# Ninety-six unused bytes at the right end of SBUF: an adaLN attention and MLP block on one core

## The chip, the core and the metric

The kernel runs on one core of a Trainium2 chip. A core has a matrix engine (TensorE, PE in the profile, with its weight loads shown apart as PEld), a vector engine (VectorE, DVE), a scalar engine (ScalarE, ACT), GpSimd (POOL) and SyncE (SP), which here issues nearly all transfers. They share an on-chip memory, SBUF, with 128 partitions; a tile takes the same bytes of every partition, so its address is a number of bytes from the start of a partition. Matrix products are accumulated in PSUM.

The metric is the device time of one execution, in microseconds (us). The kernel before takes 1168.71 us (median of three runs, 1167.72 to 1171.38).

## What is computed

There are 2048 tokens of width 576 (`x`, float32). A conditioning vector `c` gives six modulation rows. The block is linear attention with 32 heads of 18, followed by an MLP with a hidden width of 4608:

```
sa, ca, ga, sb, cb, gb = split(silu(c) @ w_mod)
h = layernorm(x) * (1 + ca) + sa
q, k, v = heads(h @ wqkv);  pq, pk = phi(q), phi(k)     # phi(t) = (t + 1 if t > 0 else exp(t)) + 1e-6
o = (pq @ (pk^T v)) / (pq @ sum(pk) + 1e-6)
x = x + ga * (o @ wo)
h = layernorm(x) * (1 + cb) + sb
x = x + gb * (silu(h @ w1) @ w2)
```

## The kernel before

**Arithmetic.** A float32 operand is kept as two parts, a rounded one (`fp32r`) and the rest, and each product takes three matmuls (high by high, high by low, low by high). PE does nearly nothing else.

**Stages.** The first stage (to about 240 us) makes the modulation, normalises and transposes `x` into the tiles `hT`, and projects K, V and half of Q, 128 tokens at a time; the weights of Q stand in the tile `wq`. The second (to about 400 us) finishes Q, applies the attention and does the first 256 hidden columns of the MLP in the plain way. The third, the main loop, does the other 17 groups of 256 hidden columns: `g` goes from 1 to 17, and for each `g` there are two units, `pair` 0 and 1, of 1024 tokens each. A short tail closes the last unit.

**A unit of the main loop.** Up and down products are done by a scheme with seven block products instead of eight. `ORDER = (1, 6, 2, 5, 7, 3, 4)` (L842) is the order of the seven. For each of them `passes` (L1211) does six matmuls, each with 128 stationary columns of a weight tile (`w`) and 512 moving columns (tokens) of an operand; products 2, 5, 3 and 4 have two more, whose stationary operand is the weights of the last 64 rows (`wt`). So there are groups of six and groups of eight. Between them stand the products of the down side, of 288 moving columns (L1284), twelve after most groups. DVE adds what they give to the accumulators (L1292), and POOL, ACT and DVE make the next operands.

**Where the moving operands come from.** Some stay in SBUF: in `hT` tiles, and, for products 7 and 3 of pair 1, in the two tiles `S`. Ten products of each `g` are streamed instead: they were stored to DRAM in tiles `hd`, and `fetch` (L968) reads each back into one of three rooms in turn. Two rooms are slices of `hT` tiles; the third is the tile `room` (L1425).

```
for room, m in rooms0.get(i) or [(rooms[(i + 2) % 3], left)]:                                  # L967
    nc.sync.dma_start(f32(room[:, :m, :]), hd[q, n][:, len(parts) : len(parts) + m, :])        # L968
...
T.matmul(ps, left, right, start=first and m == 0, stop=m == len(seq) - 1, ...)                 # L1211
```

**The tail weights.** `wts[g % 2]` holds `wt`. For odd `g` both parts lie in the tile `wtb` (L991). For even `g` they lie in the tile `wta` (L1155) and in a slice of a weight tile, which the profile calls `w`.

**Two sides of SBUF.** Pools are stacked from the left end of SBUF upwards, or, with `side="right"`, from its right end downwards. In the kernel before, the compiled program's right end lies at byte 229,344, which is 1791 times 128 and 96 over. Five pools stand there at some time, and each tile's size is a multiple of 128 bytes, so that each begins 96 bytes past a multiple of 128:

| tile (pool, line) | bytes | begins at | read by PE as |
|---|---|---|---|
| `wq` (wq, L118) | 20,736 | 208,608 | moving operand, Q projection (L212) |
| `S`, two buffers (hTb, L1059) | 8,192 each | 212,960 and 221,152 | moving operand, products 7 and 3 of pair 1 |
| `wtb` (hTb, L991) | 2,048 | 210,912 | stationary operand, odd `g` |
| `tq`, two buffers (tq, L1015) | 2,048 each | 206,816 and 208,864 | not read by PE |
| `S` (hTc, L1020) | 8,192 | 202,720 | not in the main loop |
| `room` (rs, L1425) | 10,240 | 200,672 | moving operand, a third of the streamed products |

On the left, `hT` (59,008 and 79,488), the weights `w` (99,968), `wta` (146,048), `xn` (175,744), the two tiles `first` (185,984 and 194,176) and the down weights (127,616 and up) all begin at multiples of 128.

**Order of work.** PE's order is that of the program text. From the second `g` on, the order of all engines is that of the text; between, a written list of indices for each engine (`arrange`, `ORDERS`) fixes it. Waits come from the tiles: whoever writes a tile waits for the last readers of whatever stood at the same bytes.

Of the kernel before, what the change touches and what calls it, by code (L numbers as in the profile page):

```python
# [9 lines left out]
F32 = mybir.dt.float32  # L10
# [6 lines left out]
P = 128  # L17
# [5 lines left out]
def kernel(ctx: ExitStack, tc, A_x, A_wqkv, A_wo, B_x, B_w1, B_w2, c, w_mod, out):  # L23
# [90 lines left out]
    accp = tc.alloc_tile_pool(name="acc", bufs=1)  # L114
    hTa = tc.alloc_tile_pool(name="hTa", bufs=2)
    wp = tc.alloc_tile_pool(name="w", bufs=1)
    wg = tc.alloc_tile_pool(name="wg", bufs=2)
    wqp = tc.alloc_tile_pool(name="wq", bufs=1, side="right")  # L118
    pa = tc.alloc_tile_pool(name="pa", bufs=1)
    psA = tc.alloc_tile_pool(name="psA", bufs=1, space=PSUM)  # L120
# [1020 lines left out]
    w2p = tc.alloc_tile_pool(name="w2p", bufs=1, reuse_waits="tile")  # L1141
    pu = tc.alloc_tile_pool(name="pu", bufs=1, reuse_waits="tile")
    pf = tc.alloc_tile_pool(name="pf", bufs=1, reuse_waits="tile")
    ph = tc.alloc_tile_pool(name="ph", bufs=1, reuse_waits="tile")
# [8 lines left out]
    rs = tc.alloc_tile_pool(name="rs", bufs=1, side="right", reuse_waits="tile")  # L1153
# [293 lines left out]
            unit.plain_down(work)  # L1447
            run(tokens.split(), (unit, behind2), ())
    psC.release()
    for p in (rs, ph, pf, pu, w2p, wqp, wp, hTa, accp):  # L1450
        p.release()


# [26 lines left out]
```

## Time and profile before

| | before |
|---|---|
| median of the runs | 1168.71 us (1167.72 to 1171.38) |
| profiled execution, first to last instruction | 1167.7 us |
| its mean granted TensorE clock | 0.999 |
| PE busy | 1144.4 us, 98% |
| DVE busy | 977.4 us, 84% |
| POOL busy | 660.1 us, 57% |
| ACT busy | 531.2 us, 45% |
| transferred | 268.61 MB, 230 GB/s mean |

How to read it. The span is the time from the first to the last instruction of one profiled execution; no other time of that execution is shown. A line such as `up<-room,w` names the tiles by the program's names: what is written, and after the arrow what is read; `128*128 128x512` is a stationary tile of 128 by 128 and 512 moving columns. Matmuls overlap: the duration of one includes its way through the array, so what PE pays for each is the distance from one start to the next start. In the timeline, the first column is the start of a run of like instructions, the second the time from its first start to its last end, and xN their number.

### The profile page before, as it was taken

How to read it: one execution, taken by the hardware profiler on the slowest of the kernel's cores; microseconds unless marked ns; L12 is line 12 of the kernel's file. 1: busy time of each engine (PE TensorE's matmuls, PEld its weight loads, DVE VectorE, ACT ScalarE, POOL GpSimd, SP SyncE). 2: the span in 40 equal slices, each digit the busy share in tenths (PEclk: the TensorE clock that was granted, in tenths of full speed). 3: DMA queues.
4: the chain of work that ended last, by engine and by line, in shares of the span. 5: the costliest groups of instructions: out<-in, count | busy, mean ns of one | idle time of the engine just before them, and what ended most of it. 6: DMA issues, size and time to landing. Idle time of an engine off the chain costs nothing.

```text
span 1167.7 us, 19567 instructions
## 1 busy us (share of the span) xinstructions
PE 1144.4 (98%) x7203; PEld 1058.8 (91%) x7203; DVE 977.4 (84%) x1539; ACT 531.2 (45%) x1088; POOL 660.1 (57%) x749
## 2 busy tenths in 40 slices
PE   6899999999999999999999999999999999999998
PEld 6799999999998889999999999999999999999998
DVE  3857574478797899999999999999999999999996
ACT  3553433346556454444444454444444444444541
POOL 2500000164554387677677767757767776776686
PEclk9999999999999999999999999999999999999999
DMA  8303210022357879769769779688697697697684
GB/s 284 102 28 105 64 55 1 1 83 63 112 218 266 322 261 348 274 254 351 272 252 363 266 280 334 262 319 308 249 352 275 257 345 273 255 364 268 256 308 152
DMA packets 57231, 268.61 MB, mean 230 GB/s; under 512 B 5484, under 2 KB 19312, under 8 KB 34096
## 3 DMA queue, kind: packets, MB, share of 16 engines
q1 hardware_dynamic: 56964, 267.06, 62.2%
q8 instruction: 57, 0.93, 0.3%
q10 hardware_dynamic: 172, 0.30, 0.1%
q14 instruction: 38, 0.31, 0.1%
HBM read 250.56 MB, written 16.78 MB: 229 GB/s over the span
## 4 chain that ended last, share of the span: by engine, by line
PE 94%; DVE 2%; DMA 2%; ACT 1%; issue 0%; SPq 0%; DVEq 0%; ACTq 0%
PE up L1211 33%; PE down L1284 31%; PE psK L212 12%; PE big L212 7%; PE small L774 2%; PE big L785 2%; PE kvp L517 1%; PE kvp L329 1%; PE psK L668 1%; PE big L700 1%; DMA room<-hd 1%; DVE hT L109 1%; PE small L200 1%; DMA hT<-in_w_mod_dram 1%; PE up L1314 1%; PE down L1314 1%
## 5 line engine op out<-in xcount | busy, mean ns | idle before, releaser
L1292 DVE TENSOR_TENSOR acc<-down,acc 128x576 f32<-128x576 f32 x330 | 246.2, 754 | 14.1 <-PE down L1284 4.3
L1211 PE MATMUL up<-hT,w 128*128 128x512 f32 x916 | 240.3, 391 | 0.0
L1211 PEld LDWEIGHTS up<-hT,w 128*128 128x128 f32 x916 | 164.6, 188 | 25.8
L1246 POOL TENSOR_TENSOR s<-f,f 128x256 f32<-128x256 f32 x66 | 51.6, 782 | 163.9 <-ACT f L1227 163.9
L1284 PE MATMUL down<-w,hc 128*128 128x288 f32 x792 | 120.7, 294 | 0.0
L1284 PE MATMUL down<-w,hb 128*128 128x288 f32 x792 | 120.7, 294 | 0.0
L1284 PEld LDWEIGHTS down<-w,hb 128*128 128x128 f32 x792 | 113.5, 188 | 6.0 <-DVE U L1292 0.4
L1284 PEld LDWEIGHTS down<-w,hc 128*128 128x128 f32 x792 | 113.6, 188 | 5.6
L1292 DVE TENSOR_TENSOR U<-down,U 128x576 f32<-128x576 f32 x132 | 99.5, 754 | 18.0 <-PE down L1284 15.7
L109 DVE TENSOR_TENSOR w<-v,w 128x288 fp32r<-128x288 f32 (+1 forms) x170 | 111.8, 667 | 0.4 <-ACT w L954 0.4
L212 PE MATMUL psK<-w,hT 128*128 128x288 f32 (+2 forms) x660 | 108.0, 298 | 0.8 <-DVE w L287 0.6
L212 PEld LDWEIGHTS psK<-w,hT 128*128 128x128 f32 x660 | 95.0, 189 | 1.5 <-DVE w L287 0.8
L1211 PE MATMUL up<-room,w 128*128 128x512 f32 x348 | 93.2, 396 | 1.7 <-DMA room<-hd 1.7
L1265 POOL TENSOR_TENSOR hc<-s,hc 128x512 fp32r<-128x512 f32 x66 | 89.8, 1360 | 0.0
L1227 ACT ACTIVATE f<-f 128x512 f32<-128x512 f32 x102 | 64.4, 631 | 48.1 <-DVE f L1232 25.7
L1230 DVE TENSOR_TENSOR f<-up,p 128x512 f32<-128x512 f32 x102 | 69.7, 683 | 14.7 <-PE up L1211 10.1
L1211 PEld LDWEIGHTS up<-room,w 128*128 128x128 f32 x348 | 62.4, 188 | 13.0 <-DVE f L1232 2.1
L954 ACT CAST w<-v 128x288 fp32r<-128x288 f32 x85 | 36.5, 434 | 77.0 <-PE down L1284 52.1
L1250 POOL TENSOR_TENSOR f<-f,s 128x256 f32<-128x256 f32 x66 | 50.6, 767 | 34.4 <-DVE hb L1265 27.3
L1284 PE MATMUL down<-w,hd 128*128 128x288 f32 x396 | 63.2, 295 | 0.0
L1284 PE MATMUL down<-w,he 128*128 128x288 f32 x396 | 63.1, 295 | 0.0
L1284 PE MATMUL down<-w,ha 128*128 128x288 f32 x396 | 63.0, 294 | 0.0
(284 smaller groups left out, 2498.4 us busy)
## 6 DMA issues: line engine op xcount, KB each, us to landing
hT<-hd SPq DMA_DIRECT2D x66, 1280.0 KB, 5.8
hT<-hd SPq DMA_DIRECT2D x45, 1024.0 KB, 5.1
room<-hd SPq DMA_DIRECT2D x35, 1280.0 KB, 6.0
room<-hd SPq DMA_DIRECT2D x20, 1024.0 KB, 5.8
v<-in_B_w_dram SPq DMA_DIRECT2D x17, 576.0 KB, 7.3
v<-in_B_w_dram SPq DMA_DIRECT2D x17, 512.0 KB, 7.6
hd<-S SPq DMA_DIRECT2D x6, 1024.0 KB, 4.2
xt<-in_A_x_dram SPq DMA_DIRECT2D x16, 288.0 KB, 3.1
```

The lines of the kernel that those rows point to most:

```text
L109: return V.tensor_sub(lo, full, f32(hi))
L212: T.matmul(ps, xpart(a), wpart(b), start=n == 0, stop=n == len(XW) - 1)
L774: T.matmul(ps, left, right, start=n == 0, stop=n == len(seq) - 1)
L954: A.copy(self.w2[n][:, 0], src)
L1211: T.matmul(ps, left, right, start=first and m == 0, stop=m == len(seq) - 1, skip_group_check=True)
L1227: A.activation(self.f[i, k], self.f[i, k], AF.Silu)
L1230: V.tensor_add(f, self.bank[bank[1]], self.p1)
L1246: G.tensor_add(self.s[:, 0:1], half(i, 0, 1), half(i, 1, 1))
L1250: G.tensor_sub(half(i, 1, 0), half(i, 1, 0), self.s[:, 1:2])
L1265: eng.tensor_sub(t[:, :, 1, :], src, f32(t[:, :, 0, :]))
L1284: T.matmul(ps[:, p, :HALF], self.a[i, n][:, u, p * P : (p + 1) * P], self.w.w2[n][:, v], start=n in (1, 5, 7, 6) and j == 0, stop=j == 2, ...
L1292: V.tensor_add(dst, ps[:, :, :HALF], dst)
```

## The change

A pool `edge` is opened on the right side ahead of `wq`, with one tile of 24 float32 per partition (96 bytes) that nothing reads or writes, and it is released at the end.

```diff
     wg = tc.alloc_tile_pool(name="wg", bufs=2)
+    edge = tc.alloc_tile_pool(name="edge", bufs=1, side="right")
+    edge.tile([P, 24], F32, name="edge")
     wqp = tc.alloc_tile_pool(name="wq", bufs=1, side="right")
...
-    for p in (rs, ph, pf, pu, w2p, wqp, wp, hTa, accp):
+    for p in (rs, ph, pf, pu, w2p, wqp, edge, wp, hTa, accp):
         p.release()
```

Every tile of the right side moves down by 96 bytes: `wq` to 208,512, `S` to 212,864 and 221,056, `wtb` to 210,816, `tq` to 206,720 and 208,768, the third `S` to 202,624, `room` to 200,576. All are multiples of 128. Nothing moves on the left side, whose tiles end at 200,576 or lower while `room` stands, and no instruction is added or taken away.

## The prediction

> **What bounds the kernel now.** I read the page's busy times and its chain first, then the table of stages, then the groups by shape, and last the timeline of single products.
>
> ```profile
> PE 1144.4 (98%) x7203; PEld 1058.8 (91%) x7203; DVE 977.4 (84%) x1539; ACT 531.2 (45%) x1088; POOL 660.1 (57%) x749
> PE 94%; DVE 2%; DMA 2%; ACT 1%; issue 0%; SPq 0%; DVEq 0%; ACTq 0%
> ```
> ```profile
> core 0: us, PE busy (x) PEld busy (x) DVE busy (x) ACT busy (x) POOL busy (x), PEclk, DMA share, GB/s
> 330.00:417.00 87.00, 84.52 (x520) 76.11 (x519) 75.79 (x128) 48.45 (x92) 38.65 (x42) 1.00 0.78 291
> 417.00:700.00 283.00, 283.00 (x1680) 256.31 (x1679) 263.05 (x390) 130.82 (x283) 202.90 (x241) 1.00 0.78 291
> 700.00:1000.00 300.00, 300.00 (x1781) 272.09 (x1781) 278.75 (x411) 137.38 (x298) 215.66 (x255) 1.00 0.80 298
> ```
>
> PE is 94% of the chain that ends last. In the main loop it is busy in 283.00 of 283 us and in 300.00 of 300, at the full granted clock (1.00): it waits for nobody. DVE, next, is busy in 263.05 of the 283 us, 93%. So the time of this loop is the sum of the distances between matmul starts, and nothing else. A change that moves tiles without touching an instruction can win or lose time here only by changing those distances.
>
> Do they depend on the tile? The groups by shape give the duration of one matmul behind the bar, in ns:
>
> ```profile
> L1211 PE MATMUL up<-hT,w 128*128 128x512 f32 x916 | 240.3, 391 | 0.0
> L1284 PE MATMUL down<-w,hc 128*128 128x288 f32 x792 | 120.7, 294 | 0.0
> L1211 PE MATMUL up<-room,w 128*128 128x512 f32 x348 | 93.2, 396 | 1.7 <-DMA room<-hd 1.7
> L1211 PE MATMUL up<-S,w 128*128 128x512 f32 x204 | 53.1, 395 | 0.0
> L1211 PE MATMUL up<-hT,wtb 128*128 128x512 f32 x108 | 33.5, 391 | 0.0
> L1211 PE MATMUL up<-room,wtb 128*128 128x512 f32 x34 | 10.7, 395 | 0.0
> L1211 PE MATMUL up<-first,w 128*128 128x512 f32 x12 | 2.9, 390 | 0.0
> L1314 PE MATMUL down<-w2B,hc 128*128 128x288 f32 x12 | 2.3, 296 | 0.0
> ```
>
> With the moving operand in a tile of the left side (`hT`, `first`) one takes 390 to 391 ns; in a tile of the right side (`room`, `S`) 395 to 396. That a stationary `wtb` costs anything doesn't show in durations. What PE pays is the distance of starts, which the timeline of PE shows by groups:
>
> ```profile
> 703.06 1.53 PE L1211 MATMUL up<-hT,w 128*128 128x512 f32 x6
> 704.42 0.96 PE L1284 MATMUL down<-w,hb 128*128 128x288 f32 x6
> ...
> 706.00 1.57 PE L1211 MATMUL up<-room,w 128*128 128x512 f32 x6
> ...
> 707.87 0.95 PE L1284 MATMUL down<-w,hc 128*128 128x288 f32 x6
> ...
> 709.48 1.53 PE L1211 MATMUL up<-hT,w 128*128 128x512 f32 x6
> ...
> 711.30 0.96 PE L1284 MATMUL down<-w,ha 128*128 128x288 f32 x6
> ...
> 735.48 1.57 PE L1211 MATMUL up<-S,w 128*128 128x512 f32 x6
> 736.89 0.29 PE L1284 MATMUL down<-w,hb 128*128 128x288 f32 x1
> ...
> 754.70 1.54 PE L1211 MATMUL up<-hT,w 128*128 128x512 f32 x6
> ...
> 756.53 0.95 PE L1284 MATMUL down<-w,ha 128*128 128x288 f32 x6
> ...
> 758.12 1.56 PE L1211 MATMUL up<-room,w 128*128 128x512 f32 x6
> 759.51 1.74 PE L1284 MATMUL down<-w,hb 128*128 128x288 f32 x12
> ...
> 767.93 1.54 PE L1211 MATMUL up<-hT,w 128*128 128x512 f32 x6
> 769.31 0.96 PE L1284 MATMUL down<-w,hd 128*128 128x288 f32 x6
> ...
> 841.72 1.56 PE L1211 MATMUL up<-room,w 128*128 128x512 f32 x6
> 843.58 0.95 PE L1284 MATMUL down<-w,hc 128*128 128x288 f32 x6
> ```
>
> The time of a group is the start of the first down matmul behind it less its own start. Six from `hT`: 704.42 - 703.06 = 1.36 us. Six from `S`: 736.89 - 735.48 = 1.41; from `room`: 759.51 - 758.12 = 1.39. Eight with `hT` and `wta`: 711.30 - 709.48 = 1.82. Eight with `room` and `wta`: 707.87 - 706.00 = 1.87; with `room` and `wtb`: 843.58 - 841.72 = 1.86. Eight with `hT` and `wtb`, 756.53 - 754.70 = 1.83. The other groups of a kind repeat these within 0.02. So a right-side tile costs PE in either place, as moving and as stationary operand. The one property that all of them share, and no tile of the other kind has, is a start 96 bytes past a multiple of 128.
>
> **The change part by part.** What it removes is that remainder. It adds no instruction, no transfer and no wait: every pair of tiles that shared bytes before does so after (`room` now begins exactly where the left side ends, at 200,576, and shares nothing new). I go through the reads of the right side, with the price of an all-left group as what each comes to.
>
> *Groups of six on `room` or `S`.* Of the 55 transfers into `room` 20 carry 1024 KB, for a product of six; the other 35 carry 1280 KB, for one of eight. `S` serves product 7, of six, once for each of 17 values of `g`. That is 37 groups at 1.40 (the mean of 1.39 and 1.41) against 1.36: 37 x 0.04 = 1.5 us.
>
> *Groups of eight on `room` or `S`.* 35 by `room` and 17 by product 3 on `S`: 52 at 1.87 against 1.82: 52 x 0.05 = 2.6; the 26 of odd `g` are nearer 1.86, so 2.5.
>
> *Groups of eight on `hT` with `wtb`.* The 108 matmuls with `hT` and `wtb` stand in 54 groups; 9 of these move `S` in their first six and are counted above, and one group moves `xn`: 46 are left. At 1.83 to 1.85 against 1.82, 46 x 0.02 = 0.9.
>
> *What follows such a group.* An all-left six can be dear behind a right-side group: 769.31 - 767.93 = 1.38 against 1.36. I count some 25 of the 65 all-left sixes: 25 x 0.015 = 0.4. The twelve down matmuls behind an eight with `room` and `wta` take 709.48 - 707.87 = 1.61; those behind an all-left six take 706.00 - 704.42 = 1.58. There are 26 such (18 on `room`, 8 on `S`): 26 x 0.03 = 0.8, and I take off 0.2 for the down groups behind `wtb`, which are 3 ns quicker than the others now. Together 1.0.
>
> *`wq`.* The Q projection of 128 tokens is 28 matmuls of 288 columns that move `wq`; the K projection is the same with left-side weights.
>
> ```profile
> 140.05 3.89 PE L212 MATMUL psK<-wq,hT 128*128 128x288 f32 x28
> 143.78 0.43 PE L212 MATMUL psK<-w,hT 128*128 128x288 f32 x2
> ```
> ```profile
> 164.53 0.43 PE L212 MATMUL psK<-w,hT 128*128 128x288 f32 x2
> ...
> 168.26 0.60 PE L200 MATMUL psT<-ident,xt 128*128 128x128 f32 x4
> ```
>
> Q takes 143.78 - 140.05 = 3.73 and K 168.26 - 164.53 = 3.73, by 28. At 288 columns the remainder costs nothing, and I take 0. The bound: 16 such projections at 0.01 either way, 0.2.
>
> *The transfers.* The refills of `room` land 6.0 and 5.8 us after issue by the page, those of `hT` 5.8 and 5.1, so the right side may be slower for DMA too. But PE is never idle in the loop for want of a refill; the one place is the first use of `room`:
>
> ```profile
> 394.59 8.36 DMA room<-hd
> ...
> 403.09 1.64 PE L1211 MATMUL up<-room,w 128*128 128x512 f32 x6 [1.71 <-DMA room<-hd]
> ```
>
> There 1.71 us of idle could shrink by at most the 0.7 us of the larger difference. The transfer is long because others share the queue, so I take 0 and keep 0 to 0.7. The stores from `S` and the copies by ACT and DVE into right-side tiles lie in the 330 to 417 us stage; no pair of rows separates their side from their neighbours, and I take 0.
>
> The sum: 1.5 + 2.5 + 0.9 + 1.0 = 5.9 us. Against the profiled execution that is 1167.7 - 5.9 = 1161.8; its span lies 1.0 under the median of the runs shown, so for a median I write 1168.7 - 5.9 = 1162.8 us, 0.5% less. Bounds: from below, if only the difference of the durations were won, (348 + 204) x 5 ns = 2.8 us, as 396 or 395 goes to 391; I hold to the starts because in a loop where PE is never idle they are the time. From above, 5.9 + 0.7 + 0.2 = 6.8.
>
> Does the gain reach the end? DVE would have to fill: 263.05 us in a stretch that shrinks from 283 to about 280.7 is 94%. The next bound lies 20 us away, the gain is 2.3.
>
> One rule speaks against the change. The Trainium skill, "SBUF — State Buffer", section "Specifications (TRN2)", gives SBUF lines of 16 bytes, with a penalty for each crossing to a new line. 96 is six such lines, so by that rule a start with remainder 96 is as good as one with remainder 0, and the sum would be 0 instead of 5.9 us. By that rule the first rival below is what happens; the trace so far disagrees, with 395 to 396 ns against 390 to 391.
>
> **The rivals.** *The place, not the remainder* (no change, 1168.7 us, within 1). The price could belong to the upper end of SBUF, or to something in how these tiles are written, and moving them by 96 bytes would leave it. For it: all tiles that are dear lie above 200,000 bytes, and none there is cheap. Against it: the two `first` tiles reach up to byte 202,368, over the first 1696 bytes of `room`, and their matmuls take 390 ns; `room` is filled by DMA, `S` by ACT and DVE, `wtb` by ACT and DVE again, with one price. Chance 7%.
>
> *A part only* (1164.5 to 1167.5). The distances inside a group depend on what went before (the 1.38 behind a right-side group), so an all-right-place stream may settle in another rhythm than the all-left groups that I took as model, or the waits take some of the gain. For it: that after-effect. Against it: units of even `g` hold runs of all-left groups at 1.36 and 1.82, such as those at 703.06 and 709.48, close behind dear ones. Chance 9%.
>
> *Slower.* After the change the right-side tiles begin 384 bytes past a multiple of 512, while every left tile that is read 512 columns wide begins 128 past one: a remainder that no row has tried at that width. For it: the tail's `w2B`, a down weight with remainder 384, at 296 ns, against 294 for the down matmuls in general. Against it: half of the down weights in the loop have 384 and half 128, and their group's mean is one 294. If such a start cost another 5 ns over what is paid now, as much as today's 96 cost over `hT`, the 400 + 204 matmuls that move `room` or `S` would lose 604 x 5 ns = 3.0 us, to 1171.7; from 6 ns each on it is more than a measurement's uncertainty. Chance 4%, of which I count 3% as measurably slower.
>
> **How the numbers follow.** A measurement of this kernel can tell about 0.3%, 3.5 us, from no change. The forecast (5.9 us, bounds 2.8 to 6.8) has 80%. Of it, I give the low end under 3.5 us, and an unlucky scatter of the runs, 4 points. So faster by over 0.3%: 76 points of the forecast and 5 of "a part only", 81%; slower: 3%; within 0.3%: the other 16%. The forecast with the scatter of the medians (1 us below, 3 above) spans 1161 to 1166. The range for 8 in 10 starts a little below the upper bound of the gain, 1160.5, and reaches into "a part only" to 1167.0.
>
> **What would show it right or wrong.** In the changed kernel `room` and `S` should stand at 390 to 391 ns; every group of six should take 1.36 and every one of eight 1.82; the down groups 1.58. `wq` stays at 3.73 for 28. PE stays at full busy time in the loop, which shortens by some 5.8 us of its 740. If the matmuls on `room` stay at 396, the place is the cause. If they fall to 391 and PE shows idle time in the loop, something else bounds it after all. If they rise, it is the remainder of 384.

## The result and the profile after

The changed kernel takes 1163.88 us (median of 6 runs, 1161.90 to 1167.69) against 1168.43 us (6 runs, 1167.72 to 1171.38) for the kernel before: a ratio of 0.9953, with a 95% interval of 0.9937 to 0.9969. The forecast was 1162.8 us. The profiled execution of the changed kernel spans 1163.1 us, 4.6 less than before's 1167.7; its own time was 1164.87 us, so that 1.8 us lie outside the span.

The page of the changed kernel, busy times and chain:

```profile
PE 1141.0 (98%) x7203; PEld 1061.1 (91%) x7203; DVE 982.3 (84%) x1539; ACT 531.3 (46%) x1088; POOL 660.9 (57%) x749
PE 93%; DVE 3%; DMA 2%; ACT 1%; issue 0%; SPq 0%; DVEq 0%; ACTq 0%
```

The table of stages of the changed kernel (start and end in us, length, then busy time and instruction count by engine, clock, DMA):

```profile
core 0: us, PE busy (x) PEld busy (x) DVE busy (x) ACT busy (x) POOL busy (x), PEclk, DMA share, GB/s
417.00:700.00 283.00, 282.94 (x1688) 257.72 (x1687) 266.54 (x393) 131.93 (x287) 204.76 (x243) 1.00 0.78 292
700.00:1000.00 300.00, 300.00 (x1795) 273.97 (x1794) 282.17 (x413) 138.04 (x299) 217.18 (x256) 1.00 0.81 302
```

PE is as full as before, at the same clock, and gets more done in the same stretch: 1688 matmuls start where 1680 did, and 1795 where 1781 did. DVE is busy in 266.54 of the 283 us, 94%.

The groups by shape of the changed kernel (behind the bar busy us and the mean ns of one, then idle time):

```profile
L1213 PE MATMUL up<-hT,w 128*128 128x512 f32 x916 | 239.4, 390 | 0.0
L1213 PE MATMUL up<-room,w 128*128 128x512 f32 x348 | 91.1, 390 | 1.2 <-DMA room<-hd 1.2
L1213 PE MATMUL up<-S,w 128*128 128x512 f32 x204 | 51.9, 390 | 0.0
```

`room` and `S` went from 396 and 395 ns to the 390 of `hT`. The timeline of PE of the changed kernel, the same kinds of groups as the prediction showed:

```profile
701.97 1.53 PE L1213 MATMUL up<-hT,w 128*128 128x512 f32 x6
703.34 0.96 PE L1286 MATMUL down<-w,hb 128*128 128x288 f32 x6
...
704.92 1.53 PE L1213 MATMUL up<-room,w 128*128 128x512 f32 x6
...
706.74 0.96 PE L1286 MATMUL down<-w,hc 128*128 128x288 f32 x6
...
708.32 1.53 PE L1213 MATMUL up<-hT,w 128*128 128x512 f32 x6
...
734.16 1.53 PE L1213 MATMUL up<-S,w 128*128 128x512 f32 x6
735.52 1.75 PE L1286 MATMUL down<-w,hb 128*128 128x288 f32 x12
...
756.60 1.53 PE L1213 MATMUL up<-room,w 128*128 128x512 f32 x6
757.96 1.75 PE L1286 MATMUL down<-w,hb 128*128 128x288 f32 x12
```

Six from `S`: 735.52 - 734.16 = 1.36 us, where it was 1.41. Six from `room`: 757.96 - 756.60 = 1.36, where it was 1.39. Eight with `room` and `wta`: 706.74 - 704.92 = 1.82, where it was 1.87. The twelve down matmuls behind that eight: 708.32 - 706.74 = 1.58, where they took 1.61. All as priced.

Where the time went over the execution shows in the start of the n-th matmul, which is the same matmul in both kernels:

```
matmul       before      after     difference (us)
first          4.91       5.37     +0.46
251st         59.42      61.11     +1.70
2501st       370.26     371.37     +1.11
4001st       627.38     626.85     -0.53
5001st       795.83     794.02     -1.80
6001st       964.49     961.37     -3.11
last        1164.18    1159.60     -4.58
```

From the 2501st matmul to the last one, 4.58 + 1.11 = 5.7 us are won, evenly. Up to the 251st, 1.7 us were lost, in a stage that waits for the first transfers. The change isn't the cause: two later kernels with the same distances between their tiles (both sides 32 past a multiple of 128, and the control of the last pair below) start this matmul at 59.29 and 59.49.

The sum by groups says the same. I take a six at 1.364, an eight at 1.817 and twelve down matmuls at 1.5825 us as the cheap price, and leave out the few groups that are more than 0.1 us off because a matmul in them started late; such sums are good to about 0.2. By these prices the loop of the kernel before pays 5.4 us above it in its `up` groups and 0.6 in its `down` groups. The changed kernel pays 0.2 and 0.0. So 5.8 us came out of exactly the groups that the forecast had counted.

### The profile page after: what moved, and what is told of

It reads as the page before. It is cut to its first block, busy times and chain, and to the rows that moved or that the text cites. A ratio compares the mean times of both kernels' runs of the same rounds, so it can differ in the third digit from the quotient of the medians.

```text
span 1163.1 us, 19567 instructions
## 1 busy us (share of the span) xinstructions
PE 1141.0 (98%) x7203; PEld 1061.1 (91%) x7203; DVE 982.3 (84%) x1539; ACT 531.3 (46%) x1088; POOL 660.9 (57%) x749
## 4 chain that ended last, share of the span: by engine, by line
PE 93%; DVE 3%; DMA 2%; ACT 1%; issue 0%; SPq 0%; DVEq 0%; ACTq 0%
PE up L1213 33%; PE down L1286 31%; PE psK L214 12%; PE big L214 7%; PE small L776 2%; PE big L787 2%; PE kvp L519 1%; PE kvp L331 1%; DVE hT L109 1%; PE psK L373 1%; PE psK L670 1%; PE big L702 1%; DMA hT<-in_w_mod_dram 1%; DMA room<-hd 1%; PE small L202 1%; PE up L1316 1%
## 5 line engine op out<-in xcount | busy, mean ns | idle before, releaser
L109 DVE TENSOR_TENSOR w<-v,w 128x288 fp32r<-128x288 f32 (+1 forms) x170 | 114.5, 683 | 0.4 <-ACT w L956 0.4
```

The source lines that it names most:

```text
L109: return V.tensor_sub(lo, full, f32(hi))
```

## The experiments

The reason that the forecast gave is a statement on each tile: a start that isn't a multiple of 128 bytes costs PE. Three rivals were open: another granularity (64 or 32 bytes), the place in SBUF, and a matter between tiles. The later runs test a statement of the last kind, which the first runs forced: what costs is the distance between the start of the moving operand and that of the stationary one.

**Starts alone.** A kernel of matmuls only, in chains of 24: two moving blocks in alternation, four stationary ones in turn, the second moving block 2048 bytes behind the first at 512 columns and 1152 at 288. One of the operands starts at the given number of bytes past a multiple of 512, the other at such a multiple. In `chain` the third number is the start of the moving operand and the fourth that of the stationary one.

```diff
+    for name, cols in (("mva", 512), ("mvb", 288), ("mvc", 256)):
+        for at in STEPS:
+            chain(name, cols, at, 0, cols)
...
+    for name, cols in (("sta", 512), ("stb", 288)):
+        for at in STEPS:
+            chain(name, cols, 0, at, cols)
```

> This kernel leaves the whole computation out: it streams chains of 24 matmuls of the loop's form over tiles of ones and stores zeros. Each chain has its moving operand, or its stationary one, at a chosen start past a multiple of 512 bytes (0, 16, 32, 48, 64, 80, 96, 112, 128, 160, 192, 224, 256, 352, 384); the widths are 512, 288 and 256. Theory (the remainder by 128 bytes sets the distance of starts): at 512 columns 226 to 227 ns at 0, 128, 256 and 384, and 231 to 238 ns at every other start; at 288 columns 130 to 134 ns at all; a stationary start off 128 bytes adds about 4 ns at 512 columns. Rival (lines of 64 bytes): 64 and 192 are as cheap as 0. Rival (the place, not the remainder): all chains of a width alike. If 0 or 256 were cheaper than 128, the left side could gain too, since its 512-wide tiles lie at 128 past a multiple of 256.

Mean distance from start to start in the steady part of each chain, from its 5th start to its 21st (ns, from the trace; ten of the fifteen starts):

```
bytes                    0     16     32     64     96    112    128    192    256    384
moving, 512 columns  226.6  231.7  233.5  228.9  233.8  231.5  232.1  233.3  226.7  232.3
stationary, 512      228.2  226.7  233.3  233.3  234.3  233.3  233.3  228.9  226.7  232.9
moving, 288          132.8  132.9  133.3  131.9  133.3  131.7  130.0  132.1  132.8  130.0
```

The size is right: 96 bytes cost 233.8 - 226.6 = 7.2 ns, and six of them 0.043 us, the forecast's 0.04. The reason fell. A moving start of 128 is as dear as most, 232.1, although it is a multiple of 128; of the starts shown only 0 and 256 are at the cheap 226.6 to 226.7. Yet `hT` starts 128 past a multiple of 256 in both kernels, and is cheap there. The Trainium skill, "SBUF — State Buffer", section "Specifications (TRN2)", has lines of 16 bytes and a price for crossing them. By that rule 96 and 128 bytes, which are whole lines, would cost nothing; here they cost 7.2 and 5.5 ns, and the measurement decides. At 288 columns 96 bytes cost 133.3 - 132.8 = 0.5 ns, which fits the nothing that `wq` was put at.

**Other remainders on the right side.** The changed kernel with a smaller pool at the end, 32 bytes (the right side then starts 64 past a multiple of 128) or 64 bytes (32 past one).

```diff
-    edge.tile([P, 24], F32, name="edge")
+    edge.tile([P, 8], F32, name="edge")      # the second kernel: [P, 16]
```

> The unused tile has 32 bytes instead of 96, so that the right side begins 64 bytes past a multiple of 128. Theory by lines of 128 bytes: as dear as before, six on room 1.39 to 1.41 us, time 1168.4 (ratio 1.00 to the kernel before). Rival by lines of 64 bytes: as cheap as with 96 bytes, six on room 1.36, 1163.5 to 1164 us (ratio 0.995 to 0.996).

> The unused tile has 64 bytes: remainder 32. Both the theory by 128 bytes and the one by 64 expect it as dear as before, six on room 1.39 to 1.41 us, ratio 1.00. If the price were that of the place (the highest 96 bytes) and falls with each byte moved, it would lie between, six on room near 1.375, 1165 to 1166 us.

Measured: 1.0008 of the kernel before (0.9991 to 1.0025) with remainder 64, and 1.0011 (1.0000 to 1.0021) with remainder 32. Neither gives anything, so neither 64 nor 32 bytes is the granularity. The timeline of the kernel with remainder 64 shows why it isn't better, though its groups are cheaper than before:

```profile
756.99 1.54 PE L1213 MATMUL up<-room,w 128*128 128x512 f32 x6
758.36 1.78 PE L1286 MATMUL down<-w,hb 128*128 128x288 f32 x12
759.98 1.54 PE L1213 MATMUL up<-hT,w 128*128 128x512 f32 x6
```

The six takes 1.37 here instead of 1.39 (1.383 in the mean of the 20 on `room`, instead of 1.404), but the twelve down matmuls behind it 759.98 - 758.36 = 1.62 instead of 1.58. Summed over the loop as above: `up` 3.9 us over the cheap price and `down` 3.8, together more than the 6.0 of the kernel before. With remainder 32 it is 5.9 and 1.5.

**`room` alone.** The kernel before, with 96 unused bytes ahead of `room` only: `room` starts at 200,576 as after the change, while `S`, `wtb` and `wq` stay where they were.

```diff
+    gap = tc.alloc_tile_pool(name="gap", bufs=1, side="right")
+    gap.tile([P, 24], F32, name="gap")
     rs = ...
```

> The kernel before, with the 96 unused bytes put between the right side's other tiles and room, so that room alone begins at a multiple of 128; S, wtb and wq stay at remainder 96. Theory (each tile pays for its own start, as the prediction's terms have it): room's share of the gain alone: 20 groups of six by 0.04, 35 of eight by 0.05, 18 sets of down matmuls behind room with wta by 0.03, 0.2 of after-effects: 3.3 us, so 1165.1 us (ratio 0.997); six on S stay at 1.40 to 1.41. Rival (the price hangs on the right side as a whole): no gain, or all of it.

Measured: 0.9970 (0.9959 to 0.9981), so 3.5 us of the whole gain. Its timeline:

```profile
707.91 1.53 PE L1213 MATMUL up<-room,w 128*128 128x512 f32 x6
...
709.72 0.96 PE L1286 MATMUL down<-w,hc 128*128 128x288 f32 x6
...
737.15 1.57 PE L1213 MATMUL up<-S,w 128*128 128x512 f32 x6
738.55 1.74 PE L1286 MATMUL down<-w,hb 128*128 128x288 f32 x12
```

The eight on `room` takes 1.81, the six on `S`, which hasn't moved, still 1.40. The price goes with each tile, and `room` is cheap although it lies in the same upper end of SBUF as before. The trace's sum is 2.8 over the cheap price in `up` and 0.0 in `down`: 3.2 us won. The remaining 2.8 are left to `S` and `wtb`.

**Distances and bases, in the kernel's own order.** A kernel of matmuls only again, now in the order in which the kernel uses its blocks: sixes of 512 columns from bases 0, 32, 96 and 128, the moving operand a given distance past the stationary one; twelves of 288 alone; and six and twelve in turn, the six always at base 0 and distance 0, the twelve at base 0 or 128.

```diff
+        for base in BASES:
+            for apart in APART:
+                turn[0] ^= 1
+                for _ in range(4):
+                    six(ups[turn[0]], base, apart)
...
+        for base in (0, 128):
+            for apart in MIX:
+                turn[0] ^= 1
+                for _ in range(4):
+                    six(ups[turn[0]], 0, 0)
+                    twelve(downs[turn[0]], base, apart)
```

> This kernel too leaves the computation out and stores zeros. It streams the loop's group of six (four times) with the stationary tile at base 0, 32, 96 or 128 past a multiple of 512 bytes, and the moving tile 0, 16, 32, 64, 96, 112, 128, 192 or 256 bytes further on; then the loop's twelve down matmuls, the moving tile 0 to 240 bytes further on by steps of 16; then both in turn, with the down side at two bases. Theory now (the distance of the moving from the stationary start, modulo 256, sets the price): at every base 1.36 us for six at distance 0 and 256, and 1.38 to 1.41 at 16 to 192, 128 among them. Rival (each start by itself, as a remainder of 128): dear at bases 32 and 96 whatever the distance, cheap at bases 0 and 128 with distances 0, 128 and 256. For the twelve down matmuls, 1.58 in the loop, there is no forecast; by the first micro run a distance of 128 could give 130.0 instead of 132 ns each, 1.56.

The timeline of this kernel; each chain is 24 matmuls, first at base 0 with distances 64, 96, 112, 128 and 192, then at base 96 with 0, 16, (32 left out,) 64, 96 and 112:

```profile
68.26 5.66 PE L43 MATMUL even<-move,stat 128*128 128x512 f32 x24
73.76 5.77 PE L43 MATMUL odd<-move,stat 128*128 128x512 f32 x24
79.37 5.71 PE L43 MATMUL even<-move,stat 128*128 128x512 f32 x24
84.92 5.73 PE L43 MATMUL odd<-move,stat 128*128 128x512 f32 x24
90.49 5.77 PE L43 MATMUL even<-move,stat 128*128 128x512 f32 x24
...
151.53 5.64 PE L43 MATMUL odd<-move,stat 128*128 128x512 f32 x24
157.02 5.72 PE L43 MATMUL even<-move,stat 128*128 128x512 f32 x24
...
168.18 5.66 PE L43 MATMUL even<-move,stat 128*128 128x512 f32 x24
173.67 5.77 PE L43 MATMUL odd<-move,stat 128*128 128x512 f32 x24
179.28 5.71 PE L43 MATMUL even<-move,stat 128*128 128x512 f32 x24
```

From start to start, distance 96 takes 79.37 - 73.76 = 5.61 us at base 0 and 179.28 - 173.67 = 5.61 at base 96. Distance 64 takes 5.50 and 5.49; 128 at base 0 takes 90.49 - 84.92 = 5.57. Distance 0 at base 96 takes 157.02 - 151.53 = 5.49, its first two sixes still dear behind the chain ahead; from the third on a six is 1.360, as at base 0. So both operands may start 96 bytes past a multiple of 128 and the six is cheap. In a stream of sixes the start of a tile by itself means nothing, and the distance, modulo 256, is what is paid for: in steady state a six takes 1.360 us at distance 0 and 256, 1.373 at 64, 1.385 to 1.395 at 128, 1.400 at 32, 96 and 192, alike at all four bases. The 1.56 that was thought possible for the twelve at a distance of 128 didn't come: it takes 1.587 alone and 1.577 in turn.

This explains the result in the main. `w` and `hT` start 128 past a multiple of 256. Before, `room`, `S` and `wtb` started 224 past one, 96 bytes off `w` and `hT`; the change puts them 128 past one, a distance of 0. That all these starts are multiples of 128 has no part in it. One case doesn't fit: `room` and `wtb` stood 0 apart before as well, yet the last two starts of the eights that join them cost 236 and 232 ns, no less than the 231 and 232 of `room` with `wta`.

**Both sides 32 past a multiple of 128.** If the distance is what counts, all tiles may be equally off. A 32-byte pool on the left, and 64 bytes at the right end instead of 96.

```diff
+    ledge = ctx.enter_context(tc.tile_pool(name="ledge", bufs=1))
+    ledge.tile([P, 8], F32, name="ledge")
...
-    edge.tile([P, 24], F32, name="edge")
+    edge.tile([P, 16], F32, name="edge")
```

> An unused tile of 32 bytes at the left end and one of 64 at the right: every tile of both sides begins 32 bytes past a multiple of 128, and 160 past one of 256. Theory of the distance: no distance differs from those of the changed kernel, six on hT, room and S at 1.36, ratio 0.995 to the kernel before. Rival (each start by itself): 1700 up matmuls pay 5 to 9 ns, 8 to 15 us above the kernel before, ratio 1.007 or more.

Measured: 0.9940 (0.9925 to 0.9955), the whole gain, with no operand of the loop's `up` products at a multiple of 128. The down side moved with the left one, so that all operands kept their distances. Its timeline:

```profile
699.70 1.53 PE L1215 MATMUL up<-hT,w 128*128 128x512 f32 x6
701.06 0.96 PE L1288 MATMUL down<-w,hb 128*128 128x288 f32 x6
...
702.65 1.53 PE L1215 MATMUL up<-room,w 128*128 128x512 f32 x6
...
704.46 0.96 PE L1288 MATMUL down<-w,hc 128*128 128x288 f32 x6
```

Six on `hT` 1.36, eight on `room` 1.81.

**The left side alone moved by 32.** The kernel before, with the left pool only: the right side stays 224 past a multiple of 256, the left one comes to 160, the distance to 64.

```diff
+    ledge = ctx.enter_context(tc.tile_pool(name="ledge", bufs=1))
+    ledge.tile([P, 8], F32, name="ledge")
```

> An unused tile of 32 bytes at the left end alone; the right side stays as in the kernel before. hT and the weights keep their distances; room, S and wtb stand 64 bytes from the left side modulo 256, as in the run with remainder 64. Theory of the distance: six on hT at 1.36 mostly, six on room 1.37 to 1.40, ratio 1.000 (0.998 to 1.003). Rival (each start by itself): all up matmuls are dear, ratio 1.01 or more.

Measured: 0.9996 (0.9987 to 1.0005). The groups repeat those of the run with remainder 64, which had the same distances from other starts: 3.9 us over the cheap price in `up` and 3.8 in `down`, as there.

**All multiples of 128, but 128 apart.** The changed kernel with the 128 bytes of `r` moved behind `w`, so that `hT` and `w` begin at multiples of 256, and the right side, `wta` and the down side 128 past one.

```diff
+    late = tc.alloc_tile_pool(name="late", bufs=1)
     wg = tc.alloc_tile_pool(name="wg", bufs=2)
...
-            r = const.tile([P, H], F32, name="r")
+            r = late.tile([P, H], F32, name="r")
```

> The changed kernel with one small tile of 128 bytes (r) moved from below the accumulators to above the weights: acc, hT and the weight tile w begin 128 bytes lower, still at multiples of 128, while room, S, wtb, wta and the down side stay. All tiles of both sides begin at multiples of 128, but room and S stand at a distance of 128 modulo 256 from w, and wta and wtb from hT. Theory of the distance: room and S at 232 ns a start again (six at 1.39 to 1.40), the tails too, 4 to 5 us lost against the changed kernel, ratio 0.998 to 1.002 to the kernel before. Rival (a multiple of 128 suffices): as the changed kernel, ratio 0.995.

Measured: 1.0017 (1.0005 to 1.0030): all tiles of the right side at multiples of 128, and slower than the kernel before. It decides against the reason of the forecast. Its timeline:

```profile
704.90 1.55 PE L1214 MATMUL up<-hT,w 128*128 128x512 f32 x6
706.29 0.96 PE L1287 MATMUL down<-w,hb 128*128 128x288 f32 x6
...
707.88 1.54 PE L1214 MATMUL up<-room,w 128*128 128x512 f32 x6
...
709.72 0.96 PE L1287 MATMUL down<-w,hc 128*128 128x288 f32 x6
```

The total came out as expected, its parts didn't. The first six matmuls on `room`, 128 from `w`, took 1.37 us (1.380 in the mean of 20) where 1.39 to 1.40 was expected. The groups of `hT` are dearer: 1.86 for eights with `wta` or `wtb`, which now lie 128 from `hT`, but also 1.39 for the six at 704.90 (1.384 in the mean of 62), although its `hT` and `w` are 0 apart. In the loop `up` pays 6.5 us and `down` 1.1.

So the distance within a pair isn't the whole price. What stands 128 from `hT` and `w` in these sixes is the down side between them. The second small kernel holds that very case: six at base 0 and twelve at base 128, in turn, each at distance 0.

```profile
466.16 1.55 PE L43 MATMUL even<-move,stat 128*128 128x512 f32 x6
467.55 1.75 PE L50 MATMUL ydown<-move,stat 128*128 128x288 f32 x12
469.13 1.55 PE L43 MATMUL even<-move,stat 128*128 128x512 f32 x6
```

The six takes 467.55 - 466.16 = 1.39 us, against 1.364 with both at base 0, and the twelve about 1.58 in both cases. Its six starts are 237, 228, 232, 231, 227 and 232 ns apart; those of the sixes on `hT` in this kernel 237, 228, 232, 231, 226 and 233. So the starts of neighbouring groups relative to each other count too. In the changed kernel `w`, `hT`, `wta`, the right side and both operands of the down side all begin at the same place modulo 256.

**The down matmuls, put to use.** The small kernel had shown one distance at which six and twelve in turn are quicker than at 0: 112 bytes for the twelve. From its timeline, a round of the four at distance 0 and one of the four at 112 (the six always at 0):

```profile
359.48 1.53 PE L43 MATMUL odd<-move,stat 128*128 128x512 f32 x6
360.85 1.75 PE L50 MATMUL zdown<-move,stat 128*128 128x288 f32 x12
362.43 1.53 PE L43 MATMUL odd<-move,stat 128*128 128x512 f32 x6
...
404.17 1.52 PE L43 MATMUL odd<-move,stat 128*128 128x512 f32 x6
405.53 1.72 PE L50 MATMUL zdown<-move,stat 128*128 128x288 f32 x12
407.09 1.52 PE L43 MATMUL odd<-move,stat 128*128 128x512 f32 x6
```

The twelve takes 362.43 - 360.85 = 1.58 at distance 0 and 407.09 - 405.53 = 1.56 at 112. So, in the changed kernel, the eight `w2` tiles are put into one tile, with 112 unused bytes ahead of them (and 144 behind, and a 256-byte pool ahead of `pr`; `den` and `r` leave the constant pool). A control has the same tile with the unused bytes all behind, distance 0.

```diff
+    w2s = w2p.tile([P, 28 + 8 * D + 36], F32R, name="w2")
...
-        t = w2p.tile([P, 2, HALF], F32R, name=f"w2{n}")
-        return t
...
+        i = W2.index(n)
+        return w2s[:, 28 + i * D : 28 + (i + 1) * D].rearrange("p (a d) -> p a d", a=2)
```

> The changed kernel with the eight down weights in one tile that begins with 112 unused bytes, so that the moving operand of a down matmul stands 112 bytes from its stationary one modulo 256, not 0 (two small tiles, den and r, go from the bottom of SBUF to the pools of the first stages to make room, and nothing else changes its distance). Theory of the distance, with the numbers of the run of both groups in turn (six 1360 and twelve 1560 ns at distance 112, against 1364 and 1583 at 0): 27 ns for each of some 230 pairs, 6 us under the changed kernel: ratio 0.990 to the kernel before (0.9885 to 0.992), twelve down matmuls 1.56. Rival (PE is no longer alone the bound: DVE is busy in 94% of the loop): PE shows idle time and the ratio stays over 0.993.

> The same kernel with the unused bytes behind the down weights instead of ahead of them: one tile, all moves, but distance 0 as in the changed kernel. Theory: as the changed kernel, ratio 0.995 (0.994 to 0.997), twelve down matmuls 1.58. If the single tile or the two moved tiles gained something by themselves, it would show here.

Measured: 0.9892 (0.9872 to 0.9912), 1156.03 us, with 112 bytes, and 0.9953 (0.9935 to 0.9970) for the control, the same as the change itself. The 112 bytes win 1162.88 - 1156.03 = 6.9 us over the control, and this kernel beats both the one before and the changed one. Timeline, and the stage of the loop:

```profile
706.32 1.52 PE L1216 MATMUL up<-hT,w 128*128 128x512 f32 x6
707.68 1.72 PE L1289 MATMUL down<-w,hb 128*128 128x288 f32 x12
709.24 1.52 PE L1216 MATMUL up<-room,w 128*128 128x512 f32 x6
```
```profile
417.00:700.00 283.00, 282.90 (x1704) 257.85 (x1703) 267.82 (x397) 133.71 (x289) 207.47 (x246) 1.00 0.78 293
```

The twelve takes 709.24 - 707.68 = 1.56 us. The loop's sums are 0.8 below the cheap price in `up` and 5.1 below it in `down`, 5.9 in all, so the 6 us that were expected are there and the rest of the 6.9 is within the scatter of the medians. PE stays the bound: 282.90 of 283 us, with DVE at 267.82.

**How narrow the cheap distances are.** The second small kernel in steps of 4 bytes, 216 to 292 for sixes, and around 112, 128 and 240 in turn with twelves. The cut is against the second small kernel.

```diff
-APART = (0, 16, 32, 64, 96, 112, 128, 192, 256)
...
-MIX = (0, 32, 64, 96, 112, 128, 160, 192, 224)
...
+APART = tuple(range(216, 296, 4))
...
+MIX = (0, *range(88, 136, 4), *range(224, 256, 4))
```

> Computation left out, zeros stored. Finer steps of 4 bytes: the group of six with the moving tile 216 to 292 bytes from the stationary one (which is -40 to 36 modulo 256), and six and twelve in turn with the down side 88 to 132 and 224 to 252 bytes apart. Theory of the distance says only that 256 is at 1.36; whether the cheap stretch is one point or a width of 16 bytes or more isn't known, and no number is forecast for 4-byte steps: an estimate from the first micro run, where a stationary start 16 bytes up cost nothing, is that -16 to 0 is cheap.

Its timeline, the chains at distance 240, 244, 248, 252 and 256:

```profile
85.05 5.83 PE L43 MATMUL odd<-move,stat 128*128 128x512 f32 x24
90.72 5.92 PE L43 MATMUL even<-move,stat 128*128 128x512 f32 x24
96.47 5.75 PE L43 MATMUL odd<-move,stat 128*128 128x512 f32 x24
102.06 5.66 PE L43 MATMUL even<-move,stat 128*128 128x512 f32 x24
107.55 5.61 PE L43 MATMUL odd<-move,stat 128*128 128x512 f32 x24
```

At 240 a chain takes 90.72 - 85.05 = 5.67 us and at 244 5.75, the dearest; at 252, 107.55 - 102.06 = 5.49. A steady six is 1.420 at 240, 1.440 at 244, 1.373 at 252, 1.360 at 256 and 1.423 at 260. The estimate that all of 240 to 256 is cheap was wrong: it came from the first small kernel, where a stationary start of 16, a distance of -16, cost 226.7 ns; in the kernel's order of blocks the same distance costs 236.7. So the order of the blocks matters too, beside the distance. Of the twenty distances 256 alone is at 1.360, and 4 bytes to either side are dearer; the next best is 284, at 1.367. In turn with sixes, 112 bytes is again the best for the twelve (1.560), with 108 at 1.573 and 116 at 1.625.

## Why the prediction came out

**The bound** held. The loop is the sum of the distances between PE's starts, in the changed kernel and in the variants; even in the kernel with 112 bytes, 1.1% below the one before, DVE isn't the bound.

**The terms** held one by one. Sixes on `room` and `S` went to 1.36, eights to 1.82, the twelves behind them to 1.58. Of the 5.9 us, 5.8 show in the sum of groups, 5.7 in the starts from the 2501st matmul on, and 0.47% is 5.5 us by the ratio. `room` alone, 20 sixes and 35 eights with what follows, gave 3.5. `wq` stayed at 3.71 to 3.74 us for 28 matmuls, in ten projections of fourteen; the other four took 3.80 to 4.06, where before four took 3.81 to 4.07.

**The waits**, put at 0 with a bound of 0.7: the first use of `room` waited 1.2 us where it had been 1.71. One execution each doesn't say whether the change has a part in it.

**The time** was 1163.88 where 1162.8 stood. The medians differ by 4.55 us; two kernels with the same distances, the one with both sides 32 off and the control, came to 1162.37 and 1162.88, so such medians scatter by 1 to 1.5 us.

**The reason** was wrong. The step that failed is "The one property that all of them share, and no tile of the other kind has, is a start 96 bytes past a multiple of 128." There was a second such property: 96 bytes off the operands of the left side, modulo 256. The trace of before couldn't tell them apart, because every left-side tile of the `up` products, stationary or moving, lay 128 past a multiple of 256. With the first property alone the kernel 128 apart should have been as quick as the changed one, and at 1.0017 it was slower than the one before; the kernel with both sides off by 32 should have lost the whole gain, and had all of it. The prices were measured on groups in which all operands agree modulo 256, and the change happens to make all groups such groups: 96 bytes bring the right side to a multiple of 128 that is also 128 past a multiple of 256. That was luck. By the reason of the forecast a pool of 224 bytes would have done as well, and it would have put the right side 128 from the left one; this wasn't tried, and the kernel 128 apart is the nearest to it.

**The rivals.** The place is out, by `room` alone. A part only: no other rhythm appeared, the groups settled at the prices of the model (medians 1.364 and 1.817). The slower rival looked at the right kind of number, the start modulo 512, but again of the tile by itself: 384 is 256 from the `w` that it meets, and free. A slower outcome was possible all the same by a mechanism that the rivals lacked: operands 128 apart.

Open is what in the chip makes the distance count. The runs show that it is one between operands, that 256 bytes count as 0, and that the order of the blocks and the starts and widths of the neighbouring group matter as well; no rule here gives the price of every group. None shows the reads themselves.

## What to carry to other kernels

Where PE is never idle and its time is the sum of starts, look at the starts of the moving and the stationary operand together, modulo 256 bytes, and at those of the group next to them: in streams of sixes a matmul of 512 columns cost 226.7 ns at the best distance and 228 to 240 at others, alike at the four bases tried. A property that sorts all the cheap and dear rows of one trace isn't yet the cause; look for what else is the same in them, above all in the operand that the rows have in common. Try the distance in the kernel's own order of matmuls, since the worst one for a stream alone can be the best in turn with another.

## What the runs showed of the hardware

- A matmul's cost doesn't rise evenly with distance, and 4 bytes change it: a six at 256 bytes 1.360 us, at 252 1.373, at 260 1.423, at 244 1.440, 6% more.
- 256 bytes count as 0, 128 don't: 0 and 256 cost 1.360, 128 up to 1.395.
- A distance costs what follows too: at 64 the `room` six costs 0.01 to 0.02 us more, and the down twelve behind it 0.04 more.
- So do the starts of the neighbours: a six at distance 0 takes 1.364 us between twelves at the same base, and 1.387 between twelves 128 bytes on.
- For 288 columns the best distance isn't 0. Twelves alone take 1.587 us at 0, 1.573 at 16, 1.627 at 112, the dearest of the sixteen distances tried; in turn with sixes those at 112 take 1.560, the cheapest. A small kernel with twelves alone would have pointed the wrong way.
